# Decode attention with two heads of work: half-width strips for the whole large output projection, and a row sum in place of a TensorE product for the small one

## The chip, the cores and the metric

The kernel runs on one core of one Trainium2 chip. The metric is the device time of a run in microseconds (us). "Span" is the shorter time from the first to the last instruction in the profiled run. All runs compared here are of the fast state (none shows the longer span at a lower clock that marks a slow one) or are single looks, whose state is unknown. The ratios are of mean times of fast runs of the same rounds, so they are not quite the ratio of the medians quoted beside them.

TensorE does matrix products ("PE" in the profile, "PEld" its weight loads), VectorE is "DVE", ScalarE is "ACT", SyncE's queue that issues transfers is "SPq". A transfer "lands" when all its data has arrived in the on-chip memory (SBUF). The "granted clock" is TensorE's clock as a share of full speed.

## The reference, cut to what matters

```python
def _A_ref(x, k_cache, v_cache, wq, wo):      # 32 heads, 32768 keys each, one query row
    q = (x @ wq).reshape(...)
    p = softmax(einsum("bhqd,bhkd->bhqk", q, k_cache) * Dh ** -0.5)
    o = einsum("bhqk,bhkd->bhqd", p, v_cache)
    return o.reshape(B, Sq, H * Dh) @ wo      # (1, 4096) @ (4096, 512)
# _B_ref: the same with 8 key/value heads and a window of the last 4096 keys
return concatenate([_A_ref(...), _B_ref(...)], axis=-1)
```

Both parts end with a product of one row of 4096 numbers by a 4096x512 matrix `wo` (4 MB). "The large product" is below the projection of A, "the small product" that of B; they have the same size, and the names only follow the size of their attention parts. The inputs are 570 MB, nearly all of it the K and V of A.

## The kernel before

A loop over 32 units of A streams K and V through SBUF. B is done first, except its projection. After the loop both projections run. The weights `wo` go into two thirds of the K buffer as those become free, B's in two transfers and A's in six, with ever smaller ones at the end so that little work is left after the last:

```python
WO_CUTS = {"A": (0, 11, 19, 25, 29, 31, 32), "B": (0, 16, 32)}
...
self.load(self.kbuf[:, off + 512 * a0:off + 512 * a1], src[:, 512 * a0:512 * a1],
          self.wosem[name][part], self.free["k"][t])
```

A "row" a below is one of 32 slices of the contraction: 128 numbers of the attention output (one column of `oz`) against a 128x512 block of `wo`. `halves` does such a row as two matmuls of 256 columns on two separate column groups of the array:

```python
def halves(self, e, bank, lhsT, rhs, begin, end, only=(0, 1)):
    for i in only:
        inst = e.matmul(bank[64 * i:64 * i + 1, 0:256], lhsT=lhsT, rhs=rhs[:, 256 * i:256 * i + 256], start=begin,
                        stop=end, tile_position=(0, 64 * i), skip_group_check=True)
    return inst
```

and the tail of the kernel is:

```python
def emit_proj(self):
    top = self.WO_CUTS["A"][1]                                   # 11
    for part in range(len(self.WO_CUTS["B"]) - 1):               # B: four strips of the array in turn
        o = self.proj_part("B", part, lambda e, lhsT, rhs, a: e.matmul(
            self.S[32 * (a % 4):32 * (a % 4) + 1, :], lhsT=lhsT, rhs=rhs, start=(a < 4), stop=(a >= 28),
            tile_position=(0, 32 * (a % 4)), skip_group_check=True))
    strips = self.op("dve", lambda v: v.tensor_copy(self.pb[:, :], self.S[:, :]), o)
    rows = o = self.op("pe", lambda e: e.matmul(self.ACC[0:1, :], lhsT=self.e32[:, 0:1], rhs=self.pb[:, :], ...), ...)
    o = self.op("dve", lambda v: v.tensor_copy(self.qrow[0:1, :], self.ACC[0:1, :]), o)
    # ... store of B ...
    row = self.proj_part("A", 0, lambda e, lhsT, rhs, a: e.matmul(   # first 11 rows at full width
        self.T[1][0:1, :], lhsT=lhsT, rhs=rhs, start=(a == 0), stop=(a == top - 1), skip_group_check=True))
    row = self.op("dve", lambda v: v.tensor_copy(self.pb[0:1, :], self.T[1][0:1, :]), row, rows)
    for part in range(1, len(self.WO_CUTS["A"]) - 1):
        if part == 3:                                            # add the row of part 0 back in
            self.op("pe", lambda e: self.halves(e, self.PT, self.e32[0:1, 0:1], self.pb[0:1, :], False, False), row)
        self.proj_part("A", part, lambda e, lhsT, rhs, a: self.halves(...) if a < 31 else None)
    # ... the last row's two halves, each copied to SBUF (VectorE, ScalarE) as it ends; store of A ...
```

The small product's four strips are four partial rows that must be added. In the program the large product comes after that copy and that addition, and the chain of waits below shows it waiting for them.

## Time and profile before

| | |
|---|---|
| median of 3 runs | 1323.59 us (1322.69 to 1323.95) |
| span of the profiled run | 1321.7 us |
| TensorE busy | 968 us (73%) |
| HBM read | 570 MB at 432 GB/s |

The profile page cuts the span into 40 slices and gives the busy tenths of each. The transfer row is at 9 in all but the last:

```profile
PE   4675768777677878767787777678777667877787
...
DMA  9999999999999999999999999999999999999998
```

So the loop is at the pace of the transfers, and only what comes after the last unit of A can matter to this change. The chain of waits (start, duration, what) shows that tail. L733 is the small product, L736 and L737 the copy and the sum of its strips, L741 the 11 full-width rows, L719 the half-width rows, L726 the copy to the output row:

```profile
1309.67 3.27 PE psS L733 x32
...
1312.97 0.70 DVE pb L736
...
1313.71 1.02 PE psACC L737 x2
1314.73 2.27 PE psT L741 x11
1317.01 3.02 PE psPT L719 x42
...
1320.05 0.41 DVE out_sb L726
```

No step of it waits for a transfer. The timeline (start, duration, engine, line, operation, output and inputs, count) has the start and the end of it in more detail (it counts from the first matmul on, the chain from what released the step), and, in the second fence, the issue of A's six `wo` transfers:

```profile
1309.61 3.31 PE L733 MATMUL psS<-kbuf,oz_B 128*1 128x512 bf16 x32
...
1318.57 0.59 PE L719 MATMUL psPT<-pb,e 1*1 1x256 f32 x4
...
1319.09 0.93 PE L719 MATMUL psPT<-kbuf,oz_A 128*1 128x256 bf16 x14
1320.05 0.41 DVE L726 CAST out_sb<-psPT 1x256 bf16<-1x256 f32 x1 [2.23 <-PE psPT L719]
...
1320.55 0.25 SPq L755 DMA_DIRECT2D out_dram<-out_sb  x1
```

```profile
1284.84 2.70 SPq L326 DMA_DIRECT2D kbuf<-in_A_wo_dram  x6
```

The transfer view gives size and time from issue to landing; the first and the last of the six:

```profile
kbuf<-in_A_wo_dram SPq DMA_DIRECT2D x1, 1408.0 KB, 27.4
...
kbuf<-in_A_wo_dram SPq DMA_DIRECT2D x1, 128.0 KB, 31.7
```

The first was issued at 1284.84 and the last at 1287.1, so they land at 1312.2 and 1318.8. The last 7 rows (14 matmuls at 1319.09) ran after everything had landed. The last copy starts 1.25 us after the last landing: 1320.05 against 1318.8.

### The profile page before, as it was taken

The numbers are of one execution on the slowest core, as the hardware profiler recorded it, in microseconds if no ns is written. First come the engines' busy times: TensorE is split into PE (matmuls) and PEld (weight loads), VectorE is DVE, ScalarE is ACT, GpSimd is POOL, SyncE is SP. The second block draws the span as 40 slices with busy tenths as digits, with TensorE's granted clock in tenths as the row PEclk, the third lists the DMA queues.
The fourth block names the chain that finished last, engine by engine and source line by source line (L and its number), as shares of the span: only waits on it lengthen the run. The fifth ranks groups of instructions, "written<-read, shape, count | busy, mean of one in ns | idle before, by whom it ended". The sixth has DMA issues, their size and how long they took to land. (4 is left out here: it accounts for less than half of the span.)

```text
span 1321.7 us, 28783 instructions
## 1 busy us (share of the span) xinstructions
PE 968.2 (73%) x13243; PEld 673.7 (51%) x13243; DVE 750.7 (57%) x1341; ACT 55.1 (4%) x168; POOL 2.6 (0%) x22
## 2 busy tenths in 40 slices
PE   4675768777677878767787777678777667877787
PEld 3353446555444655544465544446554445555453
DVE  3563556664555666455566645556665456665563
ACT  0000000000000000000000000000000000000000
POOL 0000000000000000000000000000000000000000
PEclk9886788887878888787888878888887788888788
DMA  9999999999999999999999999999999999999998
GB/s 404 434 434 431 440 434 434 434 436 432 433 436 436 428 438 434 428 438 434 428 442 430 428 442 432 430 438 434 437 432 432 438 430 434 438 428 436 436 428 365
DMA packets 13359, 570.59 MB, mean 432 GB/s; under 512 B 1570, under 2 KB 1700, under 8 KB 2084
## 3 DMA queue, kind: packets, MB, share of 16 engines
q1 hardware_dynamic: 13060, 570.43, 99.8%
q8 instruction: 8, 0.13, 0.0%
q10 hardware_dynamic: 288, 0.00, 0.0%
q14 instruction: 3, 0.02, 0.0%
HBM read 570.43 MB, written 0.00 MB: 432 GB/s over the span
## 5 line engine op out<-in xcount | busy, mean ns | idle before, releaser
L557 DVE COPY kt<-psT 128x1024 bf16<-128x1024 bf16 x1056 | 654.3, 683 | 236.9 <-PE psT L553 235.5
L553 PE MATMUL psT<-ident,kbuf 128*128 128x128 bf16 x8448 | 577.8, 234 | 169.0 <-DMA kbuf<-in_A_k_cache_dram 154.4
L553 PEld LDWEIGHTS psT<-ident,kbuf 128*128 128x128 bf16 x8448 | 538.1, 106 | 261.2 <-DMA kbuf<-in_A_k_cache_dram 162.5
L656 PE MATMUL psACC<-vbuf,ptsb 128*4 128x512 bf16 (+1 forms) x2112 | 187.0, 531 | 22.8 <-ACT ptsb L631 22.0
L576 PE MATMUL psS<-kt,qw 128*32 128x512 bf16 x2048 | 157.7, 385 | 14.9 <-DVE kt L557 14.9
L670 DVE TENSOR_SCALAR oc_A<-psACC,hot_A 128x128 f32<-128x128 f32 x32 | 11.2, 350 | 251.9 <-PE psG L683 251.9
L656 PEld LDWEIGHTS psACC<-vbuf,ptsb 128*4 128x4 bf16 (+1 forms) x2112 | 59.8, 111 | 140.4 <-issue 93.1
L604 ACT ACTIVATE psb<-psS,nb_A 128x512 bf16<-128x512 f32 x32 | 22.0, 687 | 1166.5 <-DVE nb_A L603 1166.5
L576 PEld LDWEIGHTS psS<-kt,qw 128*32 128x32 bf16 x2048 | 34.0, 95 | 57.6 <-DVE kt L557 30.8
L683 PE MATMUL psG<-oc_A,hw 128*32 128x128 f32 (+1 forms) x128 | 19.3, 227 | 52.3 <-DVE oc_A L672 52.3
L683 PEld LDWEIGHTS psG<-oc_A,hw 128*32 128x32 f32 x128 | 11.4, 109 | 62.4 <-DVE oc_A L672 55.0
L628 PE MATMUL psPT<-ident,psb 128*128 128x128 bf16 x136 | 18.3, 279 | 34.0 <-ACT psb L604 34.0
L672 DVE SCALAR_TENSOR_TENSOR oc_A<-psACC,hot_A,oc_A 128x128 f32<-128x128 f32 x96 | 33.6, 350 | 3.4
L593 DVE TENSOR_REDUCE tr_in<-psS 128x1 f32<-128x512 f32 x34 | 23.5, 692 | 17.2 <-PE psS L576 17.2
L628 PEld LDWEIGHTS psPT<-ident,psb 128*128 128x128 bf16 x136 | 10.3, 119 | 37.1 <-ACT psb L604 36.7
L597 PE MATMUL psACC<-rows,tr_in 128*1 128x64 f32 x64 | 8.7, 217 | 25.6 <-DVE tr_in L593 25.6
L631 ACT ACTIVATE ptsb<-psPT 128x512 bf16<-128x512 bf16 x34 | 20.3, 597 | 30.9 <-PE psPT L628 30.9
L597 PEld LDWEIGHTS psACC<-rows,tr_in 128*1 128x1 f32 x64 | 2.7, 81 | 35.1 <-DVE tr_in L593 35.1
L601 PE MATMUL psACC<-mr_A,nscale 1*128 1x1 f32 x64 | 12.1, 256 | 9.8 <-DVE mr_A L600 9.8
L601 PEld LDWEIGHTS psACC<-mr_A,nscale 1*128 1x128 f32 x64 | 9.4, 182 | 15.8 <-DVE mr_A L600 15.8
L603 DVE COPY nb_A<-psACC 128x1 f32<-128x1 f32 x32 | 5.0, 157 | 15.1 <-PE psACC L601 15.1
L600 DVE TENSOR_REDUCE mr_A<-psACC 1x1 f32<-1x64 f32 x32 | 6.8, 213 | 11.7 <-PE psACC L597 11.7
(82 smaller groups left out, 74.9 us busy)
## 6 DMA issues: line engine op xcount, KB each, us to landing
kbuf<-in_A_k_cache_dram SPq DMA_DIRECT2D x4, 4096.0 KB, 23.2
kbuf<-in_B_k_cache_dram SPq DMA_DIRECT2D x2, 4096.0 KB, 31.6
vbuf<-in_B_v_cache_dram SPq DMA_DIRECT2D x2, 4096.0 KB, 25.4
vbuf<-in_B_wq_dram SPq DMA_DIRECT2D x1, 4096.0 KB, 12.4
vbuf<-in_A_wq_dram SPq DMA_DIRECT2D x1, 4096.0 KB, 31.9
kbuf<-in_B_wo_dram SPq DMA_DIRECT2D x2, 2048.0 KB, 33.1
kbuf<-in_A_wo_dram SPq DMA_DIRECT2D x1, 1408.0 KB, 27.4
kbuf<-in_A_wo_dram SPq DMA_DIRECT2D x1, 1024.0 KB, 29.5
```

The lines of the kernel that those rows point to most:

```text
L553: inst = e.transpose(T[:, 128 * k:128 * k + 128], src[:, DH * k:DH * k + DH], self.ident[:, :])
L557: self.copies.append(self.op("dve", lambda v: v.tensor_copy(KT[:, :], T[:, :]), o, to="pe"))
L576: inst = e.matmul(self.S[32 * c:32 * c + 32, :], lhsT=win, rhs=self.kt[(bb + c // 2) % NKT][:, 512 * (c % 2):512 * (c % 2) + 512], start=b ...
L593: o = dve(lambda v: v.reduce_max(tr["in"][:, 0:1], self.S[:, :], axis=AXX), self.sdone, self.k_pool, to="pe" if name == "A" else None)
L597: o = self.op("pe", lambda e: e.matmul(self.ACC[0:1, 0:64], lhsT=tr["in"][:, 0:1], rhs=self.rows64[:, :], start=True, stop=True, skip_grou ...
L601: o = self.op("pe", lambda e: e.matmul(self.ACC[:, 64:65], lhsT=self.nscale[:, :], rhs=t["mr"][0:1, :], start=True, stop=True, skip_group_ ...
L604: self.sread = self.op("act", lambda s: s.activation(out=self.psb[:, :], in_=self.S[:, :], func=ACTF.Exp, bias=t["nb"][:, k:k + 1], scale= ...
L628: inst = e.transpose(PT[:, 128 * jj:128 * jj + 128], self.psb[:, 128 * jj:128 * jj + 128], self.ident[:, :])
L631: self.ptread = self.op("act", lambda s: s.activation(out=self.ptsb[:, :], in_=PT[:, 0:512], func=ACTF.Copy), self.psread, to="pe")
L656: inst = e.matmul(acc[32 * c:32 * c + rows, 0:512], lhsT=lhsT, rhs=rhs, start=begin, stop=end, tile_position=(0, 32 * c), skip_group_check ...
L672: o = self.op("dve", lambda v, src=src, hot=hot: v.scalar_tensor_tensor(out=oc, in0=src, scalar=hot, in1=oc, op0=ALU.mult, op1=ALU.add), p ...
L683: return self.op("pe", lambda e: e.matmul(self.G[0:32, c0 + c:c0 + c2], lhsT=win, rhs=t["oc"][g % len(t["oc"])][:, c:c2], start=False, sto ...
```

## The change

Its intent is to take work off TensorE in the tail. The strips of the small product are added by VectorE with the help of ScalarE (two rows copied by ScalarE, one by VectorE, three adds); TensorE goes straight on to the large product. All of that product runs in half-width pairs, so no separate full-width row has to be added back. The memset of `hw` moves up among the constants; `pb` is gone; one dependency list is only written otherwise.

```diff
+    def sum_strips(self, o):
+        S = [self.S[32 * c:32 * c + 1, :] for c in range(STRIPS)]
+        row = [self.kt[c][0:1, :].bitcast(F32) for c in range(STRIPS)]
+        dve = lambda fn, *deps: self.op("dve", fn, *deps)
+        act = lambda c: self.op("act", lambda e: e.activation(out=row[c], in_=S[c], func=ACTF.Copy), two)
+        add = lambda out, a, b, *deps: dve(lambda v: v.tensor_tensor(out=out, in0=a, in1=b, op=ALU.add), *deps)
+        two = self.op("dve", lambda v: v.tensor_copy(row[2], S[2]), o, to="act")
+        one, three = act(1), act(3)
+        x = add(row[0], S[0], row[1], o, one)
+        y = add(row[2], row[2], row[3], two, three)
+        return add(self.qrow[0:1, :], row[0], row[2], x, y)
...
-        strips = self.op("dve", lambda v: v.tensor_copy(self.pb[:, :], self.S[:, :]), o)
-        rows = o = self.op("pe", lambda e: e.matmul(self.ACC[0:1, :], lhsT=self.e32[:, 0:1], rhs=self.pb[:, :], ...
-        o = self.op("dve", lambda v: v.tensor_copy(self.qrow[0:1, :], self.ACC[0:1, :]), o)
+        for part in range(2):
+            o = self.emit_proj_b(part)
+        o = self.sum_strips(o)
...
-        row = self.proj_part("A", 0, lambda e, lhsT, rhs, a: e.matmul(self.T[1][0:1, :], ...
-        row = self.op("dve", lambda v: v.tensor_copy(self.pb[0:1, :], self.T[1][0:1, :]), row, rows)
-        for part in range(1, len(self.WO_CUTS["A"]) - 1):
-            if part == 3:
-                self.op("pe", lambda e: self.halves(e, self.PT, self.e32[0:1, 0:1], self.pb[0:1, :], False, False), row)
-            self.proj_part("A", part, lambda e, lhsT, rhs, a: self.halves(e, self.PT, lhsT, rhs, a == top, False)
+        for part in range(len(self.WO_CUTS["A"]) - 1):
+            self.proj_part("A", part, lambda e, lhsT, rhs, a: self.halves(e, self.PT, lhsT, rhs, a == 0, False)
                            if a < 31 else None)
```

(Cuts are marked by dots.)

More of the change, by code (lines that the diff above doesn't have):

```diff
@@ L284, in alloc @@
         self.m4 = sb("m4", [1, 128], F32)
-        self.pb = sb("pb", [128, 512], F32)
         self.out_sb = sb("out_sb", [1, 512], BF16)
@@ L456, in constants @@
             pattern=[[-32, 4], [-1, 16]], compare_op=ALU.is_equal, fill=0.0, base=0, channel_multiplier=1), rows)
+        self.k_hw = pool(lambda g: g.memset(self.hw[:, :], 0.0))
         pool(lambda g: g.memset(self.nscale[:, :], -self.SCALE))
@@ L460, in constants @@
             self.k_pool = pool(lambda g, n=n: g.memset(c[n]["b"][:, :], 0.0))
-        self.k_hw = pool(lambda g: g.memset(self.hw[:, :], 0.0))
         dve = lambda fn, *deps, **k: self.op("dve", fn, *deps, **k)
@@ L684, in emit_gather @@
             self.G[0:32, c0 + c:c0 + c2], lhsT=win, rhs=t["oc"][g % len(t["oc"])][:, c:c2], start=False, stop=True,
-            skip_group_check=True), self.accread, self.sread, self.hcopy if name == "A" else self.k_sel, to="dve")
+            skip_group_check=True), *(self.accread, self.sread, self.hcopy if name == "A" else self.k_sel), to="dve")
     def emit_spread(self, name):
@@ L727, in store @@
         return self.op("act", lambda e: e.activation(out=out, in_=src, func=ACTF.Copy), dep)
-    def emit_proj(self):
-        top = self.WO_CUTS["A"][1]
-        for part in range(len(self.WO_CUTS["B"]) - 1):
-            o = self.proj_part("B", part, lambda e, lhsT, rhs, a: e.matmul(
-                self.S[32 * (a % 4):32 * (a % 4) + 1, :], lhsT=lhsT, rhs=rhs, start=(a < 4), stop=(a >= 28),
-                tile_position=(0, 32 * (a % 4)), skip_group_check=True))
-        strips = self.op("dve", lambda v: v.tensor_copy(self.pb[:, :], self.S[:, :]), o)
-        rows = o = self.op("pe", lambda e: e.matmul(self.ACC[0:1, :], lhsT=self.e32[:, 0:1], rhs=self.pb[:, :], start=True,
-                                             stop=True, skip_group_check=True), strips, self.accread)
-        o = self.op("dve", lambda v: v.tensor_copy(self.qrow[0:1, :], self.ACC[0:1, :]), o)
-        self.op("sp", lambda e: e.dma_start(self.out[0, :, 512:1024], self.qrow[0:1, :]).then_inc(self.outsem["B"], 16), o)
-        row = self.proj_part("A", 0, lambda e, lhsT, rhs, a: e.matmul(
-            self.T[1][0:1, :], lhsT=lhsT, rhs=rhs, start=(a == 0), stop=(a == top - 1), skip_group_check=True))
-        row = self.op("dve", lambda v: v.tensor_copy(self.pb[0:1, :], self.T[1][0:1, :]), row, rows)
-        for part in range(1, len(self.WO_CUTS["A"]) - 1):
-            if part == 3:
-                self.op("pe", lambda e: self.halves(e, self.PT, self.e32[0:1, 0:1], self.pb[0:1, :], False, False), row)
-            self.proj_part("A", part, lambda e, lhsT, rhs, a: self.halves(e, self.PT, lhsT, rhs, a == top, False)
@@ new lines, in emit_proj_b @@
+    def emit_proj_b(self, part):
+        return self.proj_part("B", part, lambda e, lhsT, rhs, a: e.matmul(
+            self.S[32 * (a % 4):32 * (a % 4) + 1, :], lhsT=lhsT, rhs=rhs, start=(a < 4), stop=(a >= 28),
+            tile_position=(0, 32 * (a % 4)), skip_group_check=True))
+    def sum_strips(self, o):
[9 more added lines that the diff above has]
+        return add(self.qrow[0:1, :], row[0], row[2], x, y)
```

## The prediction

> **What bounds the kernel now.** Transfers. On the profile page the DMA row is 9 in 39 of 40 slices, mean 432 GB/s for 570 MB; TensorE is 73% busy. Its largest waits are 31 for the A keys (154 us). Only work after the last attention unit can be exposed. The chain of waits shows it: B's product starts 1309.67 (32 matmuls, 3.27 us), VectorE copies the strips to SBUF 1312.97 (0.70), TensorE adds them with the f32 product 1313.71 (1.02), A's first 11 rows full-width (2.27), then half-width rows with the row of part 0 added back (3.02), store copies 1320.05 (0.41), store issued 1320.55, span 1321.7.
>
> **Removed from TensorE** (timeline): the wait for the copy and the f32 strips product, 1312.95 to 1314.73, 1.78 us; part 0[...] becomes half-width pairs: the last 14 matmuls, 7 rows, took 0.93 us, 133 ns a row, so 11 rows 1.46 instead of 2.27, 0.8 less; the f32 add of the part-0 row, 1318.57 to 1319.09, 0.5. Together 3.1 us of TensorE work or wait on the chain.
>
> **But the data is not there.** Issues of A's wo (1284.84 to 1287.1, about 0.43 apart) plus their landing times in the DMA view give landings near 1312.2, 1314.7, 1316.7, 1317.8, 1318.3, 1318.8 for the six parts, and the windows view shows DMA falling to nothing after 1318.4. These loads are queued 25 us earlier and wait only for the third of kbuf, so the change cannot move them. [...] Before, TensorE reached part 3 at 1319.09 with all data landed: it bounds the tail by about 1 us only. After, TensorE starts A at about 1313, then waits for parts 1, 2, 3, perhaps 4, and for part 5 at 1318.8. The last matmul then starts near 1318.9 instead of 1319.73 (source view: first and last start). So of 3.1 us about 0.8 is gained; 2.3 becomes waiting for wo.
>
> **Added, off the chain.** Row copies and adds for B: VectorE copy (1x512 from PSUM, 0.68 measured), two ScalarE copies (512 columns, 0.60 to 0.69 measured), three adds. [...] In the dependency order that ends, as an estimate, at 1316.5; B's store goes out about 1316.6 instead of 1315.48. That is still before A's store at about 1319.7. The loop, its loads and its order are unchanged by the order view.
>
> **Prediction.** Span down 0.8 us, 1322.7 us, range 1321.5 to 1323.8; run spread before is 1.3 us, as large as the effect. Chances: faster by over 2% 0.003, same 0.994, slower 0.003.
>
> **What would show it.** Right: the f32 products gone; 64 half-width matmuls after B; TensorE idle gaps of 0.3 to 0.8 us before parts 1 to 3; the last matmul about 0.1 us after the last wo landing (near 1318.8 if the loop ends where it did); DMA rows unchanged; B's store about 1.1 us later. Wrong if: wo lands earlier than I read, so that up to 3 us is gained; the adds take so long that B's store is last;[...] or the loop, which is 98% of the time, drifts by a microsecond.

The end of the row sum at 1316.5, and with it B's store at 1316.6, was an estimate from the row copies and three adds. 1.78 + 0.8 + 0.5 us make the 3.1, and the landing leaves 0.8 of them.

## The result, and the profile after

| | before | changed |
|---|---|---|
| median of 6 runs, us | 1322.76 (1322.49 to 1323.95) | 1322.25 (1322.11 to 1323.17) |
| ratio of fast runs | | 0.9996, 95% interval 0.9983 to 1.0009 |
| span of the profiled run, us | 1321.7 | 1320.8 |

The medians differ by 0.5 us, and the interval includes no change at all. What follows is therefore read from the traces, where tenths of a microsecond can be seen, and only large differences are taken from the times.

The timeline of the changed kernel. L718 is the half-width product, L740 the adds of the strips (their row copies are cut), and the bracket tells how long the engine was idle and what ended it:

```profile
1311.24 1.90 PE L730 MATMUL psS<-kbuf,oz_B 128*1 128x512 bf16 x32
...
1312.97 1.37 PE L718 MATMUL psPT<-kbuf,oz_A 128*1 128x256 bf16 x22
...
1314.82 1.04 PE L718 MATMUL psPT<-kbuf,oz_A 128*1 128x256 bf16 x16 [0.48 <-DMA kbuf<-in_A_wo_dram]
...
1315.96 0.68 DVE L740 TENSOR_TENSOR qrow<-kt 1x512 bf16<-1x512 f32 x1
1316.67 0.32 SPq L752 DMA_DIRECT2D out_dram<-qrow  x1
...
1316.73 0.82 PE L718 MATMUL psPT<-kbuf,oz_A 128*1 128x256 bf16 x12 [0.87 <-DMA kbuf<-in_A_wo_dram]
...
1317.97 1.21 PE L718 MATMUL psPT<-kbuf,oz_A 128*1 128x256 bf16 x14 [0.42 <-DMA kbuf<-in_A_wo_dram]
...
1318.90 0.08 PEld L718 LDWEIGHTS psPT<-kbuf,oz_A 128*1 128x1 bf16 x2 [0.25 <-DMA kbuf<-in_A_wo_dram]
1319.20 0.41 DVE L725 CAST out_sb<-psPT 1x256 bf16<-1x256 f32 x1 [2.56 <-PE psPT L718]
...
1319.70 0.25 SPq L762 DMA_DIRECT2D out_dram<-out_sb  x1
```

TensorE now starts the large product right after the small one, and then waits before the weights of every later part: 11 rows, wait, 8 rows, wait, 6 rows, wait, and so on. The last weight load goes ahead at 1318.90, when the last part of `wo` is there, and the copy follows 0.30 us later. The chain of waits now has a transfer in it, where before it had none:

```profile
1288.46 29.46 DMA kbuf<-in_A_wo_dram
1317.97 1.22 PE psPT L718 x13
1319.20 0.41 DVE out_sb L725
```

The small product's sum ends at 1316.64 and its store goes out at 1316.67, three microseconds before the store of A.

Two things in this pair of profiles are not explained by the work that the change takes away. The small product took 3.31 us before (1309.61 to 1312.92) and 1.90 here, though its code is the same; and it began at 1309.61 before and at 1311.24 here. The clock explains the first. The windows view gives TensorE's granted clock (third figure from the end of a line) in stretches of a trace, here of before, then of the changed kernel:

```profile
1305.65:1309.10 3.45, 1.31 (x20) 0.54 (x12) 1.84 (x6) 0.00 (x0) 0.00 (x0) 0.99 0.98 421
1309.10:1312.50 3.40, 3.10 (x32) 1.11 (x36) 0.25 (x2) 0.00 (x0) 0.00 (x0) 0.50 0.98 417
```

```profile
1306.95:1310.36 3.41, 1.70 (x28) 0.73 (x20) 1.44 (x5) 0.00 (x0) 0.00 (x0) 0.99 1.00 426
```

In before the clock went to a half at 1309.1, just ahead of the small product, and back at 1312.5. In the changed kernel it was full from 1307.0 to the end of the product. The changes in before, found in stretches of 0.05 us, are at 1305.68, 1309.09 and 1312.50, 3.41 us apart each. What makes the clock change is not shown here; which clock the tail gets differs from run to run: experiments 9 to 11 below, the same kernel as before, ran the small product in 1.90 us.

The start goes with the clock too. From the first matmul of the last unit of A to the small product it is 33.3 to 33.8 us in the five profiles whose granted clock from 1276 to 1309 is 0.90, and 34.3 to 35.0 in the nine with 0.84 to 0.86. The kernel before shows both (0.90 in its first profile and experiment 11, 0.85 in 9 and 10), so a start that differs by a microsecond or more needs no change of the kernel.

The landings, in contrast, did not move. The changed kernel issued A's `wo` 2.3 us later, and it took that much less time:

```profile
1287.13 2.72 SPq L325 DMA_DIRECT2D kbuf<-in_A_wo_dram  x6
```

```profile
kbuf<-in_A_wo_dram SPq DMA_DIRECT2D x1, 1408.0 KB, 25.2
...
kbuf<-in_A_wo_dram SPq DMA_DIRECT2D x1, 128.0 KB, 29.4
```

1287.13 + 25.2 is 1312.3 and 1289.4 + 29.4 is 1318.8, the same as before (1312.2 and 1318.8). The transfer row is at 9 in all slices but the last. My reading, not tested by itself, is that the queue is always behind here and what is issued later only waits less (25.2 us against 27.4 for the first transfer).

### The profile page after: what moved, and what is told of

Read it like the earlier page. It is cut to its first block, busy times and chain, and to the rows that moved or that the text cites. A ratio compares the mean times of both kernels' runs of the same rounds, so it can differ in the third digit from the quotient of the medians.

```text
span 1320.8 us, 28798 instructions
## 1 busy us (share of the span) xinstructions
PE 968.0 (73%) x13248; PEld 677.4 (51%) x13248; DVE 753.3 (57%) x1342; ACT 56.4 (4%) x170; POOL 2.7 (0%) x22
## 6 DMA issues: line engine op xcount, KB each, us to landing
kbuf<-in_A_wo_dram SPq DMA_DIRECT2D x1, 1408.0 KB, 25.2
```

## The experiments

Theory L: the last output copy cannot start before the last landing of `wo` plus about 0.3 us, and otherwise starts when TensorE gets there. The changed kernel is always bound by the landing; the removed work became waiting. Rivals: W, both tails are bound by TensorE work, and the work removed was simply worth no more; D, both are bound by transfers; N, the loop drifts and the tails behave alike.

In all of them the times of the kernel before are from the same rounds: median 1323.07 (9 runs) for experiments 1 to 4, and 1322.78 (7 runs) for 5 to 8.

### 3 and 4: no `wo` of A to wait for

The large product reads B's `wo`, which has landed long before, and A's is not loaded. The result is wrong. The same edit on both kernels:

```diff
-        for n in ("B", "A"):
-            for part in range(len(self.WO_CUTS[n]) - 1):
-                self.load_wo(n, part)
+        for part in range(len(self.WO_CUTS["B"]) - 1):
+            self.load_wo("B", part)
...
-        return {"B": 0, "A": 1}[name]
+        return 0
...
-        deps = (self.wosem[name][part], 16), self.c[name]["ozop"]
+        deps = (self.wosem["B"][part if name == "B" else 1], 16), self.c[name]["ozop"]
```

(and the same semaphore for the last row). Experiment 3, on the kernel before:

> The kernel before, but the large product reads the weights of the small one (already landed) and its own weights are not loaded (wrong result on purpose, 4 of 570 MB less). Theory L (the tail of the changed kernel is bound by the landing of wo, the tail of before by TensorE): nothing in the tail of before waited for wo, so the time stays within about 0.5 us of before, and in the trace the time from the start of the small product to the start of the last output copy stays near 10.4 us. Rival W (both tails are bound by TensorE work): the same here. Rival D (the transfers bound both): about 9 us faster, the time of 4 MB at 432 GB/s.

Experiment 4, on the changed kernel:

> The changed kernel with the same edit (wrong result on purpose). Theory L: with no landing to wait for, the whole 3.1 us of removed TensorE work shows: 3.1 us faster than e3, 2.2 us faster than the changed kernel, no idle gap of TensorE within the large product, start of the small product to the start of the last output copy near 7.6 us at half clock or 6.2 at full. Rival W: the removed work was worth only 0.5 to 0.9 us anyway, so 0.5 to 0.9 us faster than e3 and no faster than the changed kernel.

Measured: 1324.18 us on before (4 runs, 1323.39 to 1324.98; ratio to before 1.0007, interval 0.9992 to 1.0022) and 1317.17 us on the changed kernel (4 runs, 1316.86 to 1318.10; ratio 0.9955, interval 0.9940 to 0.9970). The timelines of experiment 3, then of experiment 4:

```profile
1311.38 3.14 PE L732 MATMUL psS<-kbuf,oz_B 128*1 128x512 bf16 x32
...
1320.70 0.93 PE L718 MATMUL psPT<-kbuf,oz_A 128*1 128x256 bf16 x14
1321.67 0.41 DVE L725 CAST out_sb<-psPT 1x256 bf16<-1x256 f32 x1 [2.23 <-PE psPT L718]
```

```profile
1309.74 1.90 PE L729 MATMUL psS<-kbuf,oz_B 128*1 128x512 bf16 x32
...
1311.46 3.66 PE L717 MATMUL psPT<-kbuf,oz_A 128*1 128x256 bf16 x64
...
1315.16 0.41 DVE L724 CAST out_sb<-psPT 1x256 bf16<-1x256 f32 x1
```

In experiment 4 all 64 half-width matmuls run in one piece with no wait. 4 MB less to load made the kernel before no faster, so D falls. The same edit made the changed kernel 5.1 us faster than its own median (1322.25, of other rounds). Not all of that is the landing: between the two profiles the last copy moved by 4.04 us (1319.20 to 1315.16), of which 1.50 is an earlier start of the small product (1311.24 to 1309.74). The other 2.54 us is the wait for `wo` that went away. W has no such wait, so W falls: the work taken off TensorE was real, and the landing hid it.

How much work it was can be read from these two traces. From the start of the small product (1311.38 and 1309.74) to the start of the last copy (1321.67 and 1315.16) is 10.29 and 5.42 us, a difference of 4.87. Of this 1.24 is the clock, which was a half again for most of experiment 3's small product (3.14 against 1.90). The remaining 3.63 us is the removed work. I predicted 3.1.

The times of the two differ by 7.0 us, more than that: in these two profiles the small product also began 1.64 us apart. Two points stay open. I expected experiment 3 within 0.5 us of before and its median is 1.1 above, with an interval that includes no change; and experiment 4 gained 2.9 us more on the changed kernel than I expected. An early or late start of the tail and its clock are of that size, and the clock of the last unit (0.84 in experiment 3, 0.90 in 4) goes with it, as above. Unedited kernels show both clocks; whether the edit had a part in it is not shown.

In experiment 4 the last add of the strips ends at 1315.14 and the last matmul at 1315.12. So with no landing in the way the row sum on VectorE would have become the next limit, at the same moment as TensorE.

### 1 and 2: half of the change at a time

Experiment 1 has only the half-width rows; the strips are still added by TensorE:

```diff
-        row = self.proj_part("A", 0, ...full width...)
-        row = self.op("dve", ...copy to pb...)
-        for part in range(1, len(self.WO_CUTS["A"]) - 1):
-            if part == 3: ...add the row back...
+        for part in range(len(self.WO_CUTS["A"]) - 1):
+            self.proj_part("A", part, lambda e, lhsT, rhs, a: self.halves(e, self.PT, lhsT, rhs, a == 0, False)
+                           if a < 31 else None)
```

> Kernel before with one half of the change: the large product all in half-width pairs, no row added back; the strips of the small product still added by TensorE. Removes 1.3 of the 3.1 us. Theory L: the landing of the last wo part binds again, so this half alone has all or nearly all of the gain: last output copy starts 0.4 to 0.6 us after the last landing (before: 1.25, changed kernel: 0.4). Rival W: the gain is shared by work, 1.3/3.1 of it, so the copy starts about 0.9 us after the last landing. In the timed runs both lie within 0.5 us of each other and will hardly be told apart.

Experiment 2 has only the row sum (`sum_strips`), with the full-width rows and their f32 add kept:

> Kernel before with the other half: strips added by VectorE and ScalarE, the first 11 rows of the large product full width and their row added back in f32. Removes 1.8 of 3.1 us. Theory L: last output copy starts 0.4 to 0.6 us after the last landing, as in the changed kernel; so either half alone has the gain and the two do not add. Rival W: 1.8/3.1 of the gain, copy about 0.75 us after the last landing.

Measured: 1322.44 us (5 runs, ratio to before 0.9997, interval 0.9983 to 1.0010) and 1322.28 us (5 runs, 0.9995, interval 0.9981 to 1.0008). As expected, the times do not tell them apart. The traces do. The last weight load and the last copy, in experiment 1 and then in experiment 2:

```profile
1318.83 0.08 PEld L719 LDWEIGHTS psPT<-kbuf,oz_A 128*1 128x1 bf16 x2 [0.25 <-DMA kbuf<-in_A_wo_dram]
1319.14 0.41 DVE L726 CAST out_sb<-psPT 1x256 bf16<-1x256 f32 x1 [3.94 <-PE psPT L719]
```

```profile
1318.96 0.08 PEld L719 LDWEIGHTS psPT<-kbuf,oz_A 128*1 128x1 bf16 x2 [0.24 <-DMA kbuf<-in_A_wo_dram]
1319.27 0.41 DVE L726 CAST out_sb<-psPT 1x256 bf16<-1x256 f32 x1 [3.58 <-PE psPT L719]
```

In both, the last weight load waits for the transfer, and the copy follows 0.31 us after it, as in the changed kernel (0.30). W had the copy 0.9 and 0.75 us after the landing, so the traces look like L. But only experiment 1 tests it. Its small product began at 1310.76, and with the work of before (9.04 us from there to the copy at full clock, see 9 to 12) the copy would have come at 1319.80, not 1319.14. Experiment 2 began at 1309.65: before itself would have been done at 1318.69, ahead of the landing. That its half alone is enough is therefore an estimate: it removes 1.8 us, so a start at 1310.52, the latest of before's profiles, would end near 1317.8.

### 5 and 6: more work in front

The small product is done twice over, with the same result, on before (5, shown) and on the changed kernel (6, where the loop reads `range(2)`):

```diff
-        for part in range(len(self.WO_CUTS["B"]) - 1):
+        for part in (0, 1, 0, 1):
```

> Kernel before with the small product done twice over (same result): 32 more matmuls in front of the large product, 1.7 us at full clock, 3.3 at half. Theory L: TensorE has no slack there, the time grows by 1.5 to 3.5 us, and the last output copy starts that much later after the last landing. Rival N (the difference between the two kernels is drift of the loop and the tails behave alike): it grows as much here as in e6.

> Changed kernel with the same doubling. Theory L: the added work goes into the waits for wo (2.3 us of them), the time grows by at most 0.5 us if the product runs at full clock and by about 1 at half clock; the last output copy still starts within 0.6 us of the last landing (full clock). Rival W or N: it grows by 1.5 to 3.5 us, as in e5.

Measured: before with it 1324.52 us (4 runs, 1322.76 to 1326.77; ratio to before 1.0018, interval 1.0001 to 1.0035), changed kernel with it 1322.15 us (4 runs, 1321.98 to 1323.75; ratio to before 0.9998, interval 0.9982 to 1.0015), no more than the 1322.25 without it. The ratio of experiment 5 leaves out its fastest run, the profiled one; with all four it is 1.0013. So the growth in before, 1.7 us in the median, stands on few and scattered times. Its profile shows no growth: the small product began at 1308.68, earlier than in any profile of before, and the copy at 1319.45, 0.6 us after the last landing of 1318.9. What I expected, a copy that much later after the landing, is not there. What is there is the work: 1308.68 + 9.04 + 1.72 (3.62 less 1.90) is 1319.44, and the chain to the copy has no transfer in it:

```profile
1308.68 3.62 PE L733 MATMUL psS<-kbuf,oz_B 128*1 128x512 bf16 x64
...
1319.45 0.41 DVE L726 CAST out_sb<-psPT 1x256 bf16<-1x256 f32 x1 [2.23 <-PE psPT L719]
```

In experiment 6 the doubled product is followed by 38 matmuls (parts 0 and 1 in one piece, the wait between them used up), and the end is as it was:

```profile
1310.13 3.62 PE L730 MATMUL psS<-kbuf,oz_B 128*1 128x512 bf16 x64
...
1313.58 2.24 PE L718 MATMUL psPT<-kbuf,oz_A 128*1 128x256 bf16 x38
...
1318.72 0.08 PEld L718 LDWEIGHTS psPT<-kbuf,oz_A 128*1 128x1 bf16 x2 [0.26 <-DMA kbuf<-in_A_wo_dram]
1319.03 0.41 DVE L725 CAST out_sb<-psPT 1x256 bf16<-1x256 f32 x1 [1.77 <-PE psPT L718]
```

The tails do not behave alike: the same added work lies on the chain in one and fills a wait in the other. So N falls on the traces; the times, whose intervals overlap, would not do it alone. Experiment 5 also has 4.0 us between its fastest and slowest run. A start and a clock of the tail that reach the end would explain that, but only the fastest of these runs was profiled.

### 7 and 8: how the last transfers are cut

Changed kernel with `WO_CUTS["A"]` of (0, 11, 19, 25, 29, 32), and of (0, 16, 32).

> Changed kernel, the last two parts of wo loaded as one (3 rows in the last part). Theory L: the last landing binds, so what counts is when it comes and the work after it: landing unchanged or up to 0.3 us earlier (one transfer less), 2 rows more after it, +0.27 us; time within 0.4 us of the changed kernel.

> Changed kernel, wo of the large product loaded in two halves of 16 rows. Theory L: the last landing near 1318.8 of the span, perhaps up to 0.7 earlier if the small transfers are what leaves the engines half idle in the last 1.4 us, and 16 rows (2.1 us) after it: 1.3 to 2.1 us slower than the changed kernel. Rival W: same TensorE work in total, so same time.

Measured: 1322.40 us (4 runs) and 1323.82 us (4 runs, 1323.46 to 1324.75). Experiment 8 is 1.6 us above the changed kernel's median (of other rounds; its fastest run is above the changed kernel's slowest) with the same TensorE work, so what counts is the work left after the last landing. Its last part:

```profile
1318.72 1.91 PE L718 MATMUL psPT<-kbuf,oz_A 128*1 128x256 bf16 x32 [2.94 <-DMA kbuf<-in_A_wo_dram]
1320.67 0.41 DVE L725 CAST out_sb<-psPT 1x256 bf16<-1x256 f32 x1 [3.95 <-PE psPT L718]
```

The last `wo` was there at 1318.72, against 1318.90 in the changed kernel's profile and 1318.72 to 1318.96 in experiments 1, 2 and 6. Two transfers of 2 MB land no earlier than six with small ones at the end, so the cutting itself costs nothing that can be seen. In experiment 7 the copy starts 0.52 us after the last load of weights was let go, 0.22 more than in the changed kernel, for two rows more.

### 9 to 12: the same two kernels again

Both kernels unchanged, one look each, to see whether TensorE's lag in before's profile was typical.

> The kernel before, once more, for its profile. Theory L with a moving start: the start of the small product and its clock differ from run to run, and only a run that starts late or at half clock leaves TensorE behind the landing of wo. The last output copy starts at the larger of two times: last landing + 0.4, or start of the small product + 9.0 (full clock, product 1.9) or + 10.4 (half clock, 3.3). Theory L without it: always about 1.2 us after the last landing, as in the first profile.

> As the run before it: last output copy at the larger of last landing + 0.4 and small product's start + 9.0 or + 10.4.

> As the two before it: last output copy at the larger of last landing + 0.4 and small product's start + 9.0 or + 10.4.

> The changed kernel once more, on the same chip: last output copy 0.4 us after the last landing, whatever the start and the clock of the small product, since it would need a start after 1312 of the span to be late.

All ran on one chip. Measured, with the first two profiles for comparison (last landing from issue plus time to landing: 1318.8 in the first profile of each, in 9 and 11 and in 12; 1319.0 in 10):

| profile | small product starts | takes | last copy starts | start + 9.04 (half clock: + 10.44) |
|---|---|---|---|---|
| before | 1309.61 | 3.31 | 1320.05 | 1320.05 |
| 9, before | 1310.44 | 1.90 | 1319.48 | 1319.48 |
| 10, before | 1310.52 | 1.90 | 1319.56 | 1319.56 |
| 11, before | 1309.05 | 1.90 | 1319.12 | 1318.09 |
| changed | 1311.24 | 1.90 | 1319.20 | |
| 12, changed | 1311.24 | 1.90 | 1319.19 | |

The two constants are what profile 9 and the first profile show; 10 and 11 test them. 10 fits to the hundredth. In 11 TensorE would have been done at 1318.09, before the landing, and its copy is where the changed kernel's is. The timeline of 11 shows before waiting for `wo`, which its first profile never did:

```profile
1309.05 1.90 PE L733 MATMUL psS<-kbuf,oz_B 128*1 128x512 bf16 x32
...
1316.62 0.82 PE L719 MATMUL psPT<-kbuf,oz_A 128*1 128x256 bf16 x12 [0.61 <-DMA kbuf<-in_A_wo_dram]
...
1319.12 0.41 DVE L726 CAST out_sb<-psPT 1x256 bf16<-1x256 f32 x1 [3.26 <-PE psPT L719]
```

So before is bound by TensorE in some runs and by the landing in others, and the change takes away only the first. In the mean of these four profiles before's copy starts at 1319.55 ((1320.05 + 1319.48 + 1319.56 + 1319.12) / 4), and the changed kernel's at 1319.20: 0.35 us, not the 0.85 of the first pair. The starts are not equal, though: both profiles of the changed kernel began at 1311.24, later than any of before. From there before would have needed until 1320.28 (an estimate: 1311.24 + 9.04), so at that start the change is worth 1.1 us, and at the start of profile 11 nothing.

No version beat the changed kernel by more than noise. Experiments 1, 2, 6 and 7 all end at the same floor, 1322.15 to 1322.44, and none of them moves the last landing.

## Why the prediction was right or wrong

The time was right: 1322.7 predicted with a range of 1321.5 to 1323.8, 1322.25 measured. It is a weak test: the range also holds the unchanged kernel's median of 1322.76, so the time alone would have been right with a change worth nothing. The mechanism has to be judged point by point:

- **Right: the data is not there.** The prediction had TensorE waiting for parts 1, 2, 3, perhaps 4, and 5 at 1318.8. The profile shows waits of 0.48, 0.87 and 0.42 us before parts 1 to 3, and weight loads that wait for parts 4 and 5 as well; the last goes at 1318.90. Experiments 1, 4, 6 and 8 agree with the landing as the bound, and each goes against a rival; 2 agrees and tests nothing.
- **Right: the change cannot move the landings.** They stayed within 0.1 us, even with an issue 2.3 us later. In both traces the six came in the order of issue (from 1312.2 to 1318.8 before, from 1312.3 to 1318.8 after). Why they keep their place was not shown.
- **Right: the adds are off the chain.** B's store went at 1316.67, predicted 1316.6. The three adds of 512 took 678, 680 and 680 ns.
- **Mis-sized: the removed work.** "Together 3.1 us" measured 3.63. The step that failed is "7 rows, took 0.93 us, 133 ns a row". The 0.93 holds the 0.27 us that the last matmul takes to finish (each half-width matmul of before took 270 to 273 ns). Experiment 4 has 64 in 3.66 us; without the 0.27, 63 steps in 3.39 us are 54 ns each, 108 ns a row. The full-width row takes 216 (before's eleven start from 1314.57 to 1316.73), so the 11 rows lost 1.2 us and not 0.8. That is 0.4 of the 0.5 us missing; the rest is not broken down. This did not touch the time, since the landing covers it all.
- **Mis-sized: the gain.** "About 0.8 is gained" fits the two first profiles (0.85), but I took one profile of before as typical. Its tail ran its small product at half clock; three more profiles ran it at full clock and lay 0.5 to 0.9 us earlier at the last copy. The profiles give 0.35 us in the mean, the medians 0.5, and the timed runs cannot tell either from nothing.
- **The clock with the new waits.** The largest wait between parts is 0.87 us, and in both profiles of the changed kernel the granted clock was 1.00 from 1307.2 to 1320.

What the change did buy, though the time hardly shows it, is slack: by experiment 4's 5.42 us from the start of the small product, TensorE could have finished the changed kernel's profile at 1316.66, and the copy came at 1319.20. So by this estimate 2.5 us of extra work or delay are hidden there; experiment 6 tested 1.7 of it. Whether less spread of the times comes with it, these few runs don't show.

## What to carry to other kernels

Before costing work that is taken out of a tail, work out when the last input lands (issue plus time to landing) and cap the gain at the distance between that and the work that uses it. Take that distance from more than one profile: it moved here between 0.3 and 1.25 us with the start of the tail and its clock. Look also whether the landing moves with the issue at all. Here, with the transfer row at 9 in all slices but the last, it did not (issued 2.3 us later, landed within 0.1), and after that only the work that follows the last landing counted.

## What the traces leave open

- What makes TensorE's clock change. In before's first profile TensorE was busy 1.28 of the 3.41 us (1305.68 to 1309.09) after which the clock fell to a half, and in experiment 3 1.61 of 3.41 (1307.12 to 1310.53). In the changed kernel it was busy 1.65 of the 3.41 us from the clock's rise at 1307.00 on, and the clock stayed full. These three points are all that I have, no run varied this alone, and matmul ends are modelled: whether the two are connected is not shown.
- The order of matmuls in the record. Before's timeline lists half-width matmuls at 1316.30 and 1316.52, and the last two full-width ones, which come earlier in the program, at 1316.51 and 1316.73. I did not test whether this is the engine or the record.
- How the landing depends on the time of issue. Here an issue 2.3 us later left the landing within 0.1 us. From 1317.0 to 1318.4 the transfers in before's profile took 0.50 of the engines' time, against 1.00 from 1316 to 1317, and after that next to none (0.02 to 1319.0); coarser cuts (experiment 8) did not bring the landing forward, and the cause is open.
